# Attention into a feed-forward layer on one Trainium2 core: filler products taken out between the first scores, the first batch's gain moved behind its centering, and one batch's transposes moved into the next stage

## The chip, the core and the metric

The kernel is written for one core of a Trainium2 chip, and uses five of its instruction streams: TensorE (PE, with its weight loads as PEld), VectorE (DVE), ScalarE (ACT), GpSimd (POOL) and SyncE (SP). POOL does little arithmetic here; its queue issues nearly all loads from memory. SP's queue issues the DMA transposes and the stores. Each stream runs its instructions in the order in which they were written out.

The metric is the device time of one execution in microseconds (us). All times given here are of this one core.

## What is computed

```python
# attention: 8 batches, 12 heads, 448 tokens, 64 channels
scores = scale * np.matmul(q, k.transpose(0, 1, 3, 2))
attn = np.maximum(scores, 0.0) ** 2 / S
x = np.matmul(attn, v)                       # then heads side by side: (8, 448, 768)

# feed-forward over d_model = 768, d_ff = 3072
mu = np.mean(x, axis=-1, keepdims=True)
var = np.mean((x - mu) ** 2, axis=-1, keepdims=True)
xn = (x - mu) / np.sqrt(var + 1e-06) * g_ln
out = x + np.maximum(xn @ w_ch1, 0.0) @ w_ch2
```

There is no softmax: a score is clipped at zero and squared. The division by the deviation is a factor of a token, so the kernel takes it out of both products and multiplies with `rstd` at the end; what enters the first product is only the centred x times the gain g.

## The kernel before

**Tiling.** A pair is two heads (128 channels); a batch has six pairs, numbered on over all batches (pair 6 is the first of batch 1). Scores of a pair come in four blocks of 128 keys: `att_QK(i, t)` for t = 0, 1, 2 has 128 keys for both heads, and t = `NF` = 3 has the last 64 keys of pairs i and i+1 together, so two pairs take seven calls. Each call writes a score bank (`sc`, two of them) on PE, then ACT clips it into a buffer `attn` (line 292, seven buffers), then `att_square` squares it on DVE (line 295). `att_AV(i, half)` multiplies with v in two halves of two blocks each (line 314), and its second half ends with an evacuation, which scales into `xT` (line 321 on DVE, or 319 on ACT). q and k of batches 0 and 1 are transposed by PE (`att_T`, line 229, evacuated at line 266); those of later batches by a DMA transpose on SP's queue (line 253).

**Stages.** For each batch b in turn: FFN1(b), 24 tiles `ffn_1(ni)` of 12 products each (line 392) whose result ACT clips into `h` (line 394); then FFN2(b). The attention of batch b+1 is cut into *excursions* of three score calls, placed between the tiles of FFN1(b). An excursion begins with the `att_AV` of a finished pair. Before FFN1(0) comes an opening stage, `step_fine` for pairs 0 and 1, 2 and 3, 4 and 5, and then `first_end`; it does the attention of batch 0. Between its scores it has `warm_up(n)`: n products of 256 columns whose result nobody reads (line 556).

**Centering.** `mean_part(ki)` adds up minus the mean over channels by a product with a constant matrix (line 335). In the opening stage the gain is multiplied right after each evacuation (line 326: on POOL for pairs 0 to 3, on DVE for 4 and 5), and `center_part` adds mean times gain (line 358, DVE). For batch 1 ACT applies the gain (`gain`, line 338) and `center(1)` does the rest, both within `ffn_2_first`.

**FFN1(0) and FFN2(0).** `ffn_1_first` does the first four FFN1 tiles of batch 0 side by side, so that they can begin with the first centred channels (line 663). `ffn_2_first` is FFN2 of batch 0: two token tiles m, two halves dh of the output channels, each sum of 24 inner steps cut into four parts (`plain_part`, line 437). The sums rotate through two banks; a finished one is evacuated by DVE at line 423 and stored at line 416. Also in this stage DVE copies the columns of h that the next batch's first tile shares (`carry`, line 403) and adds up blocks of w2 (`w2_sums`, line 210) for the later batches, whose FFN2 uses seven products in place of eight (line 454, with its operand sums at line 448).

**Transposes of x.** FFN2 adds x in token order. `ffn_x(b, ki)` transposes 128 channels of `xT` into `x_tok` by DMA on SP's queue (line 372), and `ffn_stats` takes mean and variance from `x_tok` (lines 383 to 385, DVE). A batch has 448 tokens, which isn't a whole number of 128-token tiles: batch 1's tiles begin at column 384 of a ring of 896 columns, and so read the last 64 columns of the half that batch 0 and batch 2 use. The evacuation of batch 2's pair into `xT` therefore has to wait until batch 1's transpose of the same channels has been read out.

**Order.** Everything is written out by hand under a manual schedule: the program order of each stream is the order of the calls. On POOL's queue a load waits for the load eight places before it. `load_next` places the loads of w1 parts between the steps of the opening stage.

Of the kernel before, what the change touches and what calls it, by code (L numbers as in the profile page):

```python
# [11 lines left out]
def kernel(  # L12
# [10 lines left out]
    nc = tc.nc  # L23
# [270 lines left out]
    def att_square(i, t):  # L294
        nc.vector.tensor_mul(attn[i, t], attn[i, t], attn[i, t])  # L295

    av = {}

    def xT_of(b, ki):
        return xT[:, ki, (b % 2) * S:(b % 2 + 1) * S]  # L300

    def att_AV(i, half=None, bank=None, evac_by=None):
        b, pr = divmod(i, NPAIR)
        if half != 1:
            av[0] = (next_f() if bank is None else bank)[:, :S]
        ps = av[0]
        v_heads, v_rest = v_parts(b)
        for t in range(NJ) if half is None else range(half * 2, half * 2 + 2):
            for hh in range(2):
                if t < NF:  # L310
                    weights, values = v_heads[:, 2 * pr + hh, t * D:(t + 1) * D], attn[i, t][:, hh, :]
                else:
                    weights, values = v_rest[:, pr, row0(i, hh):row0(i, hh) + D], attn[i - i % 2, NF][:, i % 2, :]
                nc.tensor.matmul(ps[hh * D:(hh + 1) * D, :], weights, values,  # L314
                                 start=(t == 0), stop=(t == NJ - 1))
        if half == 0:
            return
        if evac_by is nc.scalar:
            nc.scalar.mul(xT_of(b, pr), ps, c2)
        else:  # L320
            nc.vector.tensor_scalar(xT_of(b, pr), ps, c2, None, op0=Alu.mult)  # L321
        if i >= PE_T * NPAIR and i % 2 and i + NPAIR < NP_ALL:
            load_v(i - 1 + NPAIR)
        if b == 0:
            eng = nc.gpsimd if pr < NPAIR - 2 else nc.vector
            eng.tensor_scalar(xc[:, pr, :], xT_of(b, pr), g_sb[:, pr:pr + 1], None, op0=Alu.mult)  # L326
        elif pr == 1:
            nc.vector.tensor_add(xs, xT_of(b, 0), xT_of(b, 1))
        elif 1 < pr < NPAIR - 1:
            nc.vector.tensor_add(xs, xs, xT_of(b, pr))  # L330
# [273 lines left out]
    def step_fine(i):  # L604

        att_QK(i, 0)
        att_T(i + 1)
        att_square(i, 0)
        att_QK(i, 1)
        att_square(i, 1)  # L610
        if i:
            att_AV(i - 1, 0)
            warm_up(1)
        else:
            warm_up(4)
        att_QK(i, 2)
        if i:
            att_AV(i - 1, 1)
            mean_part(i - 2)
        else:  # L620
            warm_up(4)
        att_square(i, 2)
        att_QK(i, NF)
        att_square(i, NF)
        if i:
            warm_up(4)
            mean_part(i - 1)
        else:
            warm_up(5)
        att_QK(i + 1, 0)  # L630
        if i + 2 < NPAIR:
            att_T(i + 2)
        else:
            warm_up(5)
        att_square(i + 1, 0)
        load_next()
        att_QK(i + 1, 1)
        att_square(i + 1, 1)
        att_AV(i, 0)
        warm_up(1)  # L640
        att_QK(i + 1, 2)
        att_AV(i, 1)
        att_square(i + 1, 2)
        warm_up(1)

    def first_end():
        i = NPAIR
        mean_part(i - 2)
        att_AV(i - 1, 0)
        att_T(i, nc.scalar.copy)  # L650
        warm_up(2)
        att_AV(i - 1, 1)
        att_QK(i, 0)
        att_QK(i, 1)
        mean_part(i - 1)

    def ffn_1_first():
        f_ps, m_ps = next_f(), next_f()
        tiles = [t[:, :S] for t in (f_ps, m_ps, spare[1], next_sc()[:, 0])]
        for ki in range(K1):  # L660
            center_part(ki, mean0)
            for ni, ps in enumerate(tiles):
                nc.tensor.matmul(ps, w1[:, ki, ni * P:(ni + 1) * P], xc[:, ki, :],
                                 start=(ki == 0), stop=(ki == K1 - 1))
        for ni, ps in enumerate(tiles):
            nc.scalar.activation(h[:, ni, CARRY:], ps, Act.Relu)
        for t in range(2):
            att_square(NPAIR, t)
        excursion(1)
# [4 lines left out]
    T_IN_FIRST = {4: 1, 7: 2, 10: 3, 13: 4, 16: 5}  # L674
    X_AT = (4, 6, 8, 10, 12, 14)
    V_AT = {21: PE_T * NPAIR + 2, 23: PE_T * NPAIR + 4}
    STATS_AT = {0: (18, 21, 23), 1: (15, 18, 21, 23), 2: (6, 9, 12, 15)}
    IN_REST = (1, 4, 7, 10, 13, 16, 19)

    def ffn_1_all(b):  # L680
        ms = tiles_of(b)
        for ni in range(NI0 if b == 0 else 0, K2):
            if b == 0 and ni == NI0:
                ffn_1_first()
            if b == 0 and ni in X_AT:
                ffn_x(b, X_AT.index(ni))
            if b == 0 and ni in V_AT:
                load_v(V_AT[ni])
            ffn_1(ni)
            flush()  # L690
            at = STATS_AT[min(b, 2)][:len(ms)]
            if ni in at:
                ffn_stats(ms[at.index(ni)])
            if b == 1 and ni in SUMS_AT:
                w2_sums(*LATE_SUMS[SUMS_AT.index(ni)])
            if b == 0:
                if ni in IN_FIRST:
                    excursion(3)
                if ni == IN_FIRST[-1] + 3:
                    next_AV(bank=spare[1])  # L700
                if ni in T_IN_FIRST:
                    att_T(NPAIR + T_IN_FIRST[ni])
            elif b < B - 1:
                if ni in IN_REST:
                    excursion(3, **(dict(third=(nc.scalar, nc.vector), evac_by=nc.scalar) if b == 1 else {}))
                if ni == IN_REST[-1] + 3:
                    flush_loads()
                    next_AV(bank=spare[1])

    SUMS_AT = (0, 3, 6, 9, 12, 15)  # L710
    LATE_SUMS = [(o, x, y, op, part)
                 for o, x, y, op in ((B_BOT, B21, B22, Alu.add), (B12, B12, B22, Alu.subtract),
                                     (B21, B21, B11, Alu.subtract)) for part in range(2)]
    def ffn_2_first():
        b = 0
        ffn_rstd(b)
        box = {}
        n = 0
        for dh in range(2):
            for half in range(2):  # L720
                for m, part in [(m, 2 * half + x) for m in range(2) for x in range(2)]:
                    plain_part(b, m, dh, part, 4, box)
                    if n == 1:
                        assert not ready
                        for ki in range(K1):
                            ffn_x(1, ki)
                    if n < K1 - 1:
                        gain(1, n)
                    if n == 3:
                        gain(1, K1 - 1)  # L730
                    if n == 4:
                        gain(1, K1 - 2)
                        for step in center(1):
                            step()
                    if n == 8:
                        carry(b)
                    if n in (9, 10):
                        w2_sums(B_SUM, B11, B22, Alu.add, n - 9)
                    if n in (12, 13):
                        w2_sums(B_TOP, B11, B12, Alu.add, n - 12)  # L740
                    n += 1

    def ffn_2_all(b):
        ffn_rstd(b)
# [30 lines left out]
    with tc.manual_schedule(engines=set(ENGINES)):  # L775
        load_heads(0, [("q", 2, 2), ("k", 2, 2), ("k last", 2, H - 2), ("q", 4, 4), ("k", 4, 4), ("v", 0, 4),
                       ("v last", 0, H), ("q", 8, 4), ("k", 8, 4), ("v", 4, 4), ("v", 8, 4)])
        load_early()
        load_heads(1, [("q", 0, 2), ("k", 0, 2), ("k last", 0, H)])
        load_w1(0)  # L780
        load_heads(1, [("q", 2, 4), ("k", 2, 4)])
        load_w1(1)
        later = [lambda: None,
                 lambda: (load_w1(2), load_heads(1, [("v", 0, H), ("v last", 0, H)])),
                 lambda: (load_heads(1, [("q", 6, 6), ("k", 6, 6)]), load_w1(3), load_w1(4))]

        def load_next():
            later.pop(0)()

        warm_up(17)  # L790
        att_T(0)
        warm_up(5)
        for i in range(0, NPAIR, 2):
            step_fine(i)
        load_w1(5)
        first_end()
        load_w2(B11, 0, 0)
        load_w2(B21, 1, 0)
        load_w2(B12, 0, 1)
        load_w2(B22, 1, 1)  # L800
        nc.gpsimd.memset(qk_ring, 0.0)
        i = PE_T * NPAIR
        load_qk(i)
        load_qk(i + 1)
        load_v(i)
        load_qk(i + 2)
        for b in range(B):
            ffn_1_all(b)
            if b == 0:
                ffn_2_first()  # L810
            else:
                ffn_2_all(b)
        flush()
# [30 lines left out]
```

## Time and profile before

| what | before |
|---|---|
| median of 5 runs | 536.6 us (534.84 to 537.17; two near 534.9, three near 536.9) |
| the profiled execution's own time | 534.9 us |
| its span, first to last instruction | 532.9 us |
| PE busy | 520.9 us, 98% of the span |
| DVE, ACT, POOL busy | 377.2, 274.1, 229.0 us |
| HBM read, written | 51.91 MB, 11.01 MB |

The span is cut into stages by the lines of the timeline: the opening stage runs to 32.48 us, FFN1(0) to 72.92, FFN2(0) to 90.66, FFN1(1) to 131.94; from there on six further batches repeat FFN2 and FFN1 at one pace (FFN1 of batch 2 from 159.8 to 197.5, of batch 3 from 225.2 to 262.9). A row of the timeline gives start and duration in us, the engine (a "q" behind it is its queue issuing a DMA), the line, the operation, what it writes and reads, how many were merged, and in brackets how long its engine had been idle and what ended that.

### The profile page before, as it was taken

To read this page: it belongs to the slowest core of one execution; us is meant where nothing else is said; L and a number is where in the kernel's file an instruction comes from. 1 tells how busy PE (TensorE), PEld (TensorE's weight loads), DVE (VectorE), ACT (ScalarE), POOL (GpSimd) and SP (SyncE) were. 2 spreads that over 40 slices of the span, in tenths; PEclk is the share of its full clock that TensorE was granted. 3 is DMA by queue.
4 is the path that set the end of the run, shared out by engine and by line. 5 is a ranking of instruction groups with operands and counts; after the bars stand their busy time and mean duration, and the time that the engine had idled before them with its cause. 6 is when DMAs were issued, how large, how long until landed. Compare 5 with 4: busy or idle time off the path is not lost.

```text
span 532.9 us, 13760 instructions
## 1 busy us (share of the span) xinstructions
PE 520.9 (98%) x5732; PEld 317.4 (60%) x5732; DVE 377.2 (71%) x660; ACT 274.1 (51%) x443; POOL 229.0 (43%) x259
## 2 busy tenths in 40 slices
PE   9989998989999999999999999999999999999996
PEld 5445567546885556655666556655666556666664
DVE  5866779767876878679684887789595876960264
ACT  6956660867327663176632776366624665234320
POOL 8937216667443574326832277228632000320021
PEclk9999999999999999999999999999999999999999
DMA  9999999999534995559934699469924200240022
GB/s 139 183 175 201 205 199 126 149 160 129 50 85 96 98 115 64 107 86 108 106 53 92 101 101 147 77 73 104 116 53 112 44 18 3 70 110 1 1 62 60
DMA packets 175230, 53.04 MB, mean 100 GB/s; under 512 B 154176, under 2 KB 175168, under 8 KB 175168
## 3 DMA queue, kind: packets, MB, share of 16 engines
q0 software_dynamic: 103552, 25.74, 52.3%
q1 hardware_dynamic: 71088, 26.06, 26.2%
q8 instruction: 45, 0.74, 0.6%
q10 hardware_dynamic: 528, 0.37, 0.2%
q14 instruction: 17, 0.14, 0.1%
HBM read 51.91 MB, written 11.01 MB: 118 GB/s over the span
## 4 chain that ended last, share of the span: by engine, by line
PE 81%; DMA 13%; POOL 3%; ACT 2%; issue 1%; DVE 0%; POOLq 0%; DVEq 0%; ACTq 0%
PE f L392 35%; PE f L454 33%; DMA qk_ring<-in_k_dram 5%; PE f L314 5%; DMA s_sb<-in_v_dram 3%; PE sc L284 3%; DMA w<-in_moe_w_ch_dram 2%; PE f L437 1%; PE f L284 1%; DMA w<-in_q_dram 1%; ACT at L292 1%; PE sc L279 1%; POOL xc L326 1%; DMA qkT_t<-qk_ring 1%; POOL w L201 0%
## 5 line engine op out<-in xcount | busy, mean ns | idle before, releaser
L392 PE MATMUL f<-xc,w 128*64 128x448 bf16 x2256 | 227.0, 354 | 0.3
L392 PEld LDWEIGHTS <-w 128*64 128x64 bf16 x2256 | 125.0, 110 | 93.6 <-issue 18.5
L394 ACT ACTIVATE h<-f 128x448 bf16<-128x448 f32 x188 | 102.6, 546 | 103.5 <-PE f L392 102.1
L454 PE MATMUL f<-w,s_sb 128*64 128x384 bf16 (+2 forms) x1584 | 130.0, 324 | 0.0
L292 ACT ACTIVATE at<-sc 128x896 bf16<-128x896 f32 x120 | 104.6, 916 | 18.5 <-PE sc L284 12.2
L454 PEld LDWEIGHTS <-s_sb 128*64 128x64 bf16 x1584 | 92.3, 110 | 35.1
L295 DVE TENSOR_TENSOR at<-at 128x896 bf16<-128x896 bf16 x168 | 97.0, 621 | 6.4 <-ACT at L292 5.7
L488 POOL TENSOR_TENSOR o_t<-o_t,x_tok 128x384 f32<-128x384 f32 x26 | 24.4, 939 | 157.4 <-ACT o_t L487 133.4
L166 POOL DMA_DIRECT2D qk_ring<-in_q_dram x36 | 44.9, 1246 | 84.4 <-DMA qkT_t<-qk_ring 77.3
L290 DVE TENSOR_SCALAR at<-f 128x448 bf16<-128x448 f32 x89 | 51.5, 617 | 25.3 <-PE f L284 25.3
L448 DVE TENSOR_TENSOR s_sb<-h 128x1536 bf16<-128x1536 bf16 x65 | 64.8, 1013 | 0.0
L487 ACT ACTIVATE o_t<-f,rstd 128x384 f32<-128x384 f32 x26 | 15.1, 581 | 94.7 <-DVE acc L492 46.8
L167 POOL DMA_DIRECT2D qk_ring<-in_k_dram x36 | 53.8, 1495 | 4.6 <-DMA w<-in_moe_w_ch_dram 4.6
L454 PE MATMUL f<-w,h 128*64 128x384 bf16 x624 | 52.9, 326 | 0.0
L168 POOL DMA_DIRECT2D qk_ring<-in_k_dram x36 | 45.3, 1258 | 6.1 <-DMA w<-in_moe_w_ch_dram 6.1
L321 DVE TENSOR_SCALAR xT<-f 128x448 bf16<-128x448 f32 x43 | 26.8, 623 | 29.7 <-PE f L314 29.6
L454 PEld LDWEIGHTS <-h 128*64 128x64 bf16 x624 | 36.6, 110 | 14.5
L314 PE MATMUL f<-at,v_ring 128*64 128x448 bf16 x336 | 40.2, 354 | 0.0
L488 POOL TENSOR_TENSOR acc<-acc,x_tok 128x384 f32<-128x384 f32 x24 | 28.1, 1178 | 22.5 <-ACT acc L487 20.8
L358 DVE SCALAR_TENSOR_TENSOR xc<-f,g_sb,xc 128x448 bf16<-128x448 f32 x48 | 30.1, 675 | 8.9 <-PE f L351 8.8
L178 POOL DMA_DIRECT2D v_ring<-in_v_dram x36 | 32.9, 1223 | 5.3 <-DMA w<-in_moe_w_ch_dram 5.0
L284 PE MATMUL sc<-qkT_t 64*128 64x448 bf16 x206 | 31.3, 356 | 0.2 <-ACT qkT_t L266 0.2
(81 smaller groups left out, 395.6 us busy)
## 6 DMA issues: line engine op xcount, KB each, us to landing
w<-in_moe_w_ch_dram POOLq DMA_DIRECT2D x6, 768.0 KB, 13.6
w<-in_moe_w_ch_dram POOLq DMA_DIRECT2D x4, 1152.0 KB, 27.1
v_ring<-in_v_dram POOLq DMA_DIRECT2D x21, 192.0 KB, 5.1
qk_ring<-in_q_dram POOLq DMA_DIRECT2D x36, 112.0 KB, 4.5
qk_ring<-in_k_dram POOLq DMA_DIRECT2D x36, 96.0 KB, 5.2
out_dram<-o_t SPq DMA_DIRECT2D x9, 168.0 KB, 2.2
out_dram<-o_t SPq DMA_DIRECT2D x9, 144.0 KB, 2.1
out_dram<-acc SPq DMA_DIRECT2D x7, 144.0 KB, 2.1
```

Of the source, the lines that this page charges most:

```text
L167: nc.gpsimd.dma_start(k_to[:, :NF], k[b, heads, :SF].rearrange("x (p t) d -> p t x d", t=NF))
L168: nc.gpsimd.dma_start(k_to[:SS, NF], k[b, 2 * a:2 * a + 2, SF:].rearrange("x s d -> s x d"))
L284: nc.tensor.matmul(by_j(half[hh]), k_of(i, r, t, P), q_of(i, r), start=True, stop=True)
L290: nc.vector.tensor_scalar(at[:, x], half[x], 0.0, None, op0=Alu.max)
L292: nc.scalar.activation(at, ps[:, :, :S], Act.Relu)
L295: nc.vector.tensor_mul(attn[i, t], attn[i, t], attn[i, t])
L314: nc.tensor.matmul(ps[hh * D:(hh + 1) * D, :], weights, values, start=(t == 0), stop=(t == NJ - 1))
L392: nc.tensor.matmul(ps[c * D:(c + 1) * D, :], w1[:, ki, n0:n0 + D], xc[:, ki, :], start=(ki == 0), stop=(ki == K1 - 1))
L394: nc.scalar.activation(h[:, ni, CARRY:], ps, Act.Relu)
L448: nc.vector.tensor_tensor(s_sb[:, n], x, y, op=op)
L454: nc.tensor.matmul(ps[c * D:(c + 1) * D, :d1 - d0], stat[:, ki, c * D:(c + 1) * D], w2[:, slot, ki, d0:d1], start=(start and ki == 0), sto ...
L488: nc.gpsimd.tensor_tensor(o_t, o_t, x_half(m, dh), op=Alu.add)
```

## The change

Five edits, all in the first three stages.

1. **Opening stage.** Of 58 filler products 33 are left: the 22 at the start stay, steps and end have 11 in place of 36. `att_AV` orders its four blocks so that an odd pair begins with the shared last block (`[NF, 0, 1, 2]`), and its halves follow that order. `mean_part` is called behind the block of last keys and not before it. The transposes of pair 6 move from `first_end` into the last step and are evacuated by DVE, no longer by ACT; `first_end` has the two halves of the last `att_AV` around the first scores of pair 6.
2. **Loads.** `load_next` is gone; all loads of w1, v, q and k are issued ahead of the steps, in the same order as before.
3. **Gain.** Only pairs 0 and 1 are multiplied with the gain right away, on DVE; POOL has no gain any more. For channels 2 to 5 `ffn_1_first` adds the mean to `xT` on DVE and then ACT multiplies with the gain.
4. **FFN2(0).** For the first half of output channels the order is now tile by tile (m = 0 with its four parts, then m = 1); the second half keeps its order. Centering of batch 1 is spread over parts 4, 6 and 8 in place of part 4 alone. Of the two block sums of w2, the one that doesn't need the last block comes first. A doubled `gain(1, 4)` is gone.
5. **Batch 1's transposes of x** move from FFN2(0), part 1, to FFN1(1), tiles 4, 6, 8, 10, 12 and 14; its statistics from tiles 15, 18, 21 and 23 to 20, 21, 22 and 23.

```diff
+    GAIN_FIRST = 2
...
-        for t in range(NJ) if half is None else range(half * 2, half * 2 + 2):
+        order = [NF, 0, 1, 2] if i % 2 else [0, 1, 2, NF]
+        for n, t in enumerate(order):
+            if half is not None and n // 2 != half:
+                continue
...
-            eng = nc.gpsimd if pr < NPAIR - 2 else nc.vector
-            eng.tensor_scalar(xc[:, pr, :], xT_of(b, pr), g_sb[:, pr:pr + 1], None, op0=Alu.mult)
+            if pr < GAIN_FIRST:
+                nc.vector.tensor_scalar(xc[:, pr, :], xT_of(b, pr), g_sb[:, pr:pr + 1], None, op0=Alu.mult)
...
             att_AV(i - 1, 0)
-            warm_up(1)
         else:
-            warm_up(4)
+            warm_up(3)
         att_QK(i, 2)
         if i:
             att_AV(i - 1, 1)
-            mean_part(i - 2)
         else:
-            warm_up(4)
+            warm_up(3)
...
         if i:
-            warm_up(4)
+            mean_part(i - 2)
+            warm_up(1)
+        else:
+            warm_up(3)
+        att_QK(i + 1, 0)
+        if i:
             mean_part(i - 1)
-        else:
-            warm_up(5)
-        att_QK(i + 1, 0)
-        if i + 2 < NPAIR:
-            att_T(i + 2)
-        else:
-            warm_up(5)
+        att_T(i + 2)
         att_square(i + 1, 0)
-        load_next()
...
     def first_end():
         i = NPAIR
+        att_AV(i - 1, 0)
+        att_QK(i, 0)
         mean_part(i - 2)
-        att_AV(i - 1, 0)
-        att_T(i, nc.scalar.copy)
-        warm_up(2)
+        att_QK(i, 1)
         att_AV(i - 1, 1)
-        att_QK(i, 0)
-        att_QK(i, 1)
         mean_part(i - 1)
...
         for ki in range(K1):
-            center_part(ki, mean0)
+            if ki < GAIN_FIRST:
+                center_part(ki, mean0)
+            else:
+                nc.vector.tensor_tensor(xc[:, ki, :], mean0, xT_of(0, ki), op=Alu.add)
+                nc.scalar.activation(xc[:, ki, :], xc[:, ki, :], Act.Identity, scale=g_sb[:, ki:ki + 1])
...
-    STATS_AT = {0: (18, 21, 23), 1: (15, 18, 21, 23), 2: (6, 9, 12, 15)}
+    STATS_AT = {0: (18, 21, 23), 1: (20, 21, 22, 23), 2: (6, 9, 12, 15)}
...
-            if b == 0 and ni in X_AT:
+            if b < 2 and ni in X_AT:
                 ffn_x(b, X_AT.index(ni))
...
+    CENTER_AT = (4, 6, 8)
...
-            for half in range(2):
-                for m, part in [(m, 2 * half + x) for m in range(2) for x in range(2)]:
-                    plain_part(b, m, dh, part, 4, box)
-                    if n == 1:
-                        assert not ready
-                        for ki in range(K1):
-                            ffn_x(1, ki)
...
-                        for step in center(1):
-                            step()
...
+            order = [(m, part) for m in range(2) for part in range(4)]
+            if dh:
+                order.sort(key=lambda x: x[1] // 2)
+            for m, part in order:
+                plain_part(b, m, dh, part, 4, box)
...
+                if n in CENTER_AT:
+                    steps[CENTER_AT.index(n)]()
...
+                if n in (9, 10):
+                    w2_sums(B_TOP, B11, B12, Alu.add, n - 9)
+                if n in (12, 13):
+                    w2_sums(B_SUM, B11, B22, Alu.add, n - 12)
```

More of the change, by code (lines that the diff above doesn't have):

```diff
@@ L314, in att_AV @@
                 nc.tensor.matmul(ps[hh * D:(hh + 1) * D, :], weights, values,
-                                 start=(t == 0), stop=(t == NJ - 1))
+                                 start=(n == 0), stop=(n == NF))
         if half == 0:
@@ L639, in step_fine @@
         att_AV(i, 0)
-        warm_up(1)
         att_QK(i + 1, 2)
@@ L643, in step_fine @@
         att_square(i + 1, 2)
-        warm_up(1)
     def first_end():
         i = NPAIR
+        att_AV(i - 1, 0)
+        att_QK(i, 0)
         mean_part(i - 2)
-        att_AV(i - 1, 0)
-        att_T(i, nc.scalar.copy)
-        warm_up(2)
+        att_QK(i, 1)
         att_AV(i - 1, 1)
-        att_QK(i, 0)
-        att_QK(i, 1)
         mean_part(i - 1)
@@ L717, in ffn_2_first @@
         box = {}
+        assert not ready
+        steps = center(1)
         n = 0
         for dh in range(2):
-            for half in range(2):
-                for m, part in [(m, 2 * half + x) for m in range(2) for x in range(2)]:
-                    plain_part(b, m, dh, part, 4, box)
-                    if n == 1:
-                        assert not ready
-                        for ki in range(K1):
-                            ffn_x(1, ki)
[L727 to L732, printed above, removed]
-                        for step in center(1):
-                            step()
[L735 to L741, printed above, removed]
+            order = [(m, part) for m in range(2) for part in range(4)]
[3 more added lines that the diff above has]
+                plain_part(b, m, dh, part, 4, box)
+                if n < K1 - 1:
+                    gain(1, n)
+                if n == 3:
+                    gain(1, K1 - 1)
+                if n in CENTER_AT:
+                    steps[CENTER_AT.index(n)]()
+                if n == 8:
+                    carry(b)
+                if n in (9, 10):
+                    w2_sums(B_TOP, B11, B12, Alu.add, n - 9)
+                if n in (12, 13):
+                    w2_sums(B_SUM, B11, B22, Alu.add, n - 12)
+                n += 1
     def ffn_2_all(b):
@@ L782 @@
         load_w1(1)
[L783 to L788, printed above, removed]
+        load_w1(2)
+        load_heads(1, [("v", 0, H), ("v last", 0, H), ("q", 6, 6), ("k", 6, 6)])
+        for c in range(3, NCH):
+            load_w1(c)
         warm_up(17)
@@ L794 @@
             step_fine(i)
-        load_w1(5)
         first_end()
```

## The prediction, made before the changed kernel had run

> **What bounds the kernel now.** The page first: PE is busy 98% of the span, at a granted clock of 0.9 or more in every slice, so the end can come earlier only where PE stands still or does work that nobody needs. The table of windows finds these places. Its columns are the busy time of PE, PEld, DVE, ACT and POOL, the clock, and DMA.
>
> ```profile
> core 0: us, PE busy (x) PEld busy (x) DVE busy (x) ACT busy (x) POOL busy (x), PEclk, DMA share, GB/s
> 25.00:30.00 5.00, 4.06 (x43) 1.65 (x41) 3.50 (x6) 2.73 (x4) 4.86 (x5) 1.00 1.52 159
> 30.00:35.00 5.00, 3.92 (x24) 1.68 (x24) 4.21 (x8) 2.45 (x3) 0.85 (x1) 1.00 1.23 198
> 80.00:85.00 5.00, 3.59 (x46) 2.75 (x43) 5.00 (x8) 0.00 (x0) 4.14 (x5) 1.00 1.66 140
> 105.00:110.00 5.00, 3.23 (x32) 1.73 (x28) 2.82 (x4) 2.51 (x6) 0.00 (x0) 1.00 1.45 272
> ```
>
> Three holes: 2.0 us around 30, 1.41 at 82, 1.77 at 108. What surrounds each is in the timeline. The opening stage:
>
> ```profile
> 16.76 6.82 ACT L292 ACTIVATE at<-sc 128x896 bf16<-128x896 f32 x7 [0.20 <-DVE xT L321]
> ...
> 23.78 3.89 ACT L292 ACTIVATE at<-sc 128x896 bf16<-128x896 f32 x4 [0.20 <-DVE xT L321]
> ...
> 27.71 0.61 DVE L321 TENSOR_SCALAR xT<-f 128x448 bf16<-128x448 f32 x1
> ...
> 28.61 0.62 DVE L295 TENSOR_TENSOR at<-at 128x896 bf16<-128x896 bf16 x1
> ...
> 30.60 0.62 DVE L321 TENSOR_SCALAR xT<-f 128x448 bf16<-128x448 f32 x1 [1.38 <-PE f L314]
> ```
>
> ACT clips scores nearly without a stop from 7.16 to 27.67 and is the stage's pace; PE's busy time here is partly filler. The last square starts 0.9 behind the last clip, since DVE evacuates pair 4 first, and pair 5 is evacuated only at 30.60. The end of FFN2(0):
>
> ```profile
> 78.64 3.64 DVE L358 SCALAR_TENSOR_TENSOR xc<-f,g_sb,xc 128x448 bf16<-128x448 f32 x6 [3.62 <-PE f L351]
> ...
> 82.86 7.99 PE L437 MATMUL f<-w,h 128*64 128x384 bf16 x96 [1.41 <-DVE o_t L423]
> ...
> 85.41 3.88 DVE L210 TENSOR_TENSOR w<-w 128x2304 bf16<-128x2304 bf16 x3
> ...
> 91.00 0.60 DVE L423 SCALAR_TENSOR_TENSOR o_t<-f,rstd,x_tok 128x384 f32<-128x384 f32 x1
> ```
>
> PE waits 1.41 for a bank, because its evacuation stands behind six centerings. But DVE then has no hole from 78.64 to 91.60. And SP's queue, whose rows are issue times:
>
> ```profile
> 82.10 10.24 SPq L253 DMA_TRANSPOSE qkT_t<-qk_ring  x3
> 92.39 8.18 SPq L372 DMA_TRANSPOSE x_tok<-xT  x6
> 100.67 5.93 SPq L416 DMA_DIRECT2D out_dram<-o_t  x8
> 106.77 21.89 SPq L253 DMA_TRANSPOSE qkT_t<-qk_ring  x6
> ```
>
> The fourth q/k transpose (pair 15) is issued at 106.77 behind six transposes of x and eight stores; PE waits for it from about 108.3 to 110.14.
>
> **Opening stage.** 21 clips at 917 ns are 19.26 us; they took 20.51. The other 1.25 are gaps in which PE was late with the next scores. A step of PE (first scores of pair 3 to those of pair 5) runs from 17.37 to 24.39: 7.02 for seven clips of 6.42 together. In it lie three single fillers at 0.22 (19.09 to the scores at 19.31) and a block of four at 0.45; one stays, so PE needs about 7.02 - 0.9 = 6.1, less than ACT. DVE's step is eleven operations at a pitch of 0.55 (18.41, 18.95), 6.05, plus 0.34 for one gain: just below ACT too, with POOL's arithmetic, beside which one square took 1089 ns against 615, out of its way. I leave 0.4 of the gaps, for the two slots that hold a mean and transposes: the last clip ends at 26.8, not 27.68. Behind it the evacuation of pair 4 is already done, its gain is gone, pair 6's transposes and the waiting mean are off the path: square 26.9 to 27.5, AV at 27.55, evacuation 0.61 later (29.99 to 30.60), 28.16. From that evacuation to the first centering was 1.15 (30.60 to 31.75) and to the first FFN1 product 0.73 more: 30.04, against 32.48. **Gain 2.4.**
>
> Added: channels 2 to 5 pass DVE and then ACT. The add has no row; nearest is the centering, 674 ns at a pitch of 607 (bounds: 0.62, as the clip of one PSUM block at line 290, to 0.69). ACT's gain is 4.14 / 7 = 0.59. Channel 2 is ready at 29.31 + 2 x 0.607 + 0.67 + 0.07 + 0.62 = 31.88; PE, at 0.757 for four products, wants it at 31.55. That is 0.3 once; later channels come every 0.61 and are used every 0.757. **Net -2.1**, bounds -1.2 (fillers only took PE's waiting time, so clips keep their pace, and the tail alone gains) to -2.8.
>
> The loads lose POOL's four gains (6.9 us) in between, but their order is the same and POOL waits for earlier loads either way, up to 80.34 for the last w2 block; hidden, 0. That block is first used in part 12 of FFN2(0), near 82.5. FFN1(0) moves as a whole; a w1 part that POOL sees landed at 53.44 is used after 56.
>
> **FFN2(0).** The bank wait goes, since tile 0's evacuation now stands ahead of centering. What is late next is DVE: its run of 12.96 has one evacuation (0.55) fewer behind the mean, which comes after the same five parts, now at 76.4; and it must wait about 0.4 for tile 1's last part. Its last evacuation ends near 76.5 + 12.4 + 0.4 = 89.4, against 91.60, which is the 2.1 already counted. FFN1(1)'s second tile needs that bank: PE stops twice for 0.7 at the stage's start in place of 1.41 at 82. **-0.1**, bounds -1.4 (a bank comes free earlier) to +0.2.
>
> **SP's queue.** The first three q/k transposes stay where the loads put them (to 92.34). Then come the stores, 8 x 0.5 to 0.74, one transpose of x from about 97, and pair 15's transpose from about 98.5. The landing of line 253 has a median of 4.3: 103, where PE wants it at 108.3 - 2.2 = 106.1. The hole of 1.77 goes; 0.2 comes back, because ACT had caught up in it. **-1.6.**
>
> A new wait: batch 2's evacuation into `xT` (line 319 on ACT, 102.86, now 100.6) must wait for batch 1's transpose of the same channels, and behind it on ACT are the clips of scores and FFN1 tiles, for which PE's banks wait. Its landing: 97 + 3.3 (as 106.77 to PE's 110.14) = 100.3, just in time; by the extremes that the view of line 372 gives for batches 0 to 2, 2.3 to 8.6 us, it is 99.3 to 105.6. I take the nearest, 0 cost; bounds 0 to +5. The later channels have 1 us or more of slack.
>
> **Statistics.** Four sets at 1.25 now follow the last excursion, whose squares end at 129.2, with one evacuation of 0.57: 134.4 to 134.8 against 132.83. From there to the end of the first operand sum is 1.40 (134.23): 135.8 to 136.2. The third product of FFN2(1) wants it at 131.94 + 2 x 1.95 = 135.84. **+0.2**, bounds 0 to 0.6.
>
> **Sum.** -2.1 - 0.1 - 1.6 + 0.2 = -3.6. Against the profiled execution's 534.9 that gives 531.3. This execution was among the two fast ones of five; their mean is 536.1 and their median 536.6. The changed kernel's runs should scatter likewise, so I take the mean less 3.6: **532.5**.
>
> [...] The trace grants a clock of 1.00 in all four windows above, three of them with PE a fifth or more idle. [...] After the change PE has, between 26.9 and 30.04, only one AV and one mean, some 0.9 us of work in 3.1; the row of before that is nearest, 106.5 to 110, had half of 3.5 busy and kept its clock. [...]
>
> **Rivals**, on the mean of 536.1:
> - *DVE doesn't bind* at the end of FFN2(0), and the 1.41 is gained whole: 531.2. For it: some of DVE's copies may shorten. Against: its unbroken run.
> - *The opening stage keeps its pace*: -2.2 or so remains: 533.9. For it: fillers fill time in which PE waits. Against: the 0.1 gaps of ACT behind nearly each clip.
> [...]
> - *Slower*: ACT stands at line 319 for batch 1's transposes, as said. At the longest landing, 8.6, ACT stops 5.0 us in the third excursion, and PE with it, for its banks: 536.1 - 3.6 + 5.0 = 537.5. It decides once the first transpose of x lands later than 100.6 + 3.6 = 104.2. Against: the long landings had up to five transposes ahead of them.
>
> **How the numbers follow.** Forecast 0.55; DVE not binding 0.12; opening stage 0.11; clock 0.10; ACT waiting 0.12. A measurement here can tell about 0.3%, 1.6 us, from no change. The forecast and the first rival are beyond that save a tenth of it, the second and third about six times in ten: faster 0.74. Slower is most of the last: 0.11; the rest 0.15. The range takes the bounds of the forecast (-2.8 - 1.6 - some of 1.4 at one end, -1.2 and a short ACT wait at the other): 529.5 to 535.5.
>
> **What would show it.** Right: clips ending near 26.8 and the first product of line 663 near 30.0; no wait at line 437, but PE waiting for line 423 at the start of FFN1(1); no wait at line 279 for line 253; a third product of FFN2(1) hardly late; clock 1.00 throughout. Wrong: a wait of line 319 on line 372, a clock below 1 between 26 and 36, or the last evacuation of FFN2(0) well ahead of PE.

## The result, and the profile after

The changed kernel takes **533.34 us** (median of 43 runs, 530.02 to 537.00), the kernel before 536.02 (80 runs, 532.49 to 538.64): a ratio of **0.9955, 95% interval 0.9943 to 0.9968**. The profiled execution took 533.51, with a span of 531.7, where that of before had 532.9. Line numbers are now those of the changed kernel: 284, 292 and 295 stay, 319, 335, 358, 372, 392, 416, 423, 437 and 663 are now 324, 340, 363, 377, 397, 421, 428, 442 and 664.

The same four windows as before:

```profile
core 0: us, PE busy (x) PEld busy (x) DVE busy (x) ACT busy (x) POOL busy (x), PEclk, DMA share, GB/s
25.00:30.00 5.00, 3.27 (x24) 1.24 (x23) 3.77 (x8) 2.78 (x4) 2.06 (x3) 1.00 1.36 174
30.00:35.00 5.00, 4.85 (x28) 2.27 (x28) 3.13 (x6) 3.46 (x7) 0.83 (x1) 1.00 1.24 198
80.00:85.00 5.00, 5.00 (x64) 3.48 (x62) 5.00 (x6) 0.00 (x0) 4.56 (x5) 1.00 1.60 152
105.00:110.00 5.00, 4.74 (x32) 2.69 (x31) 3.05 (x4) 3.68 (x7) 4.02 (x5) 0.66 1.88 200
```

The hole at 82 is gone, and the row from 30 is nearly full. But the last row has a clock of 0.66: PE is busy because it is slow. The timeline shows the gain first, at the end of the opening stage:

```profile
24.25 1.73 ACT L292 ACTIVATE at<-sc 128x896 bf16<-128x896 f32 x2 [0.40 <-PE sc L284]
...
26.22 1.80 ACT L292 ACTIVATE at<-sc 128x896 bf16<-128x896 f32 x2 [0.24 <-PE sc L284]
...
27.60 0.62 DVE L326 TENSOR_SCALAR xT<-f 128x448 bf16<-128x448 f32 x1 [0.71 <-PE f L319]
...
29.40 0.73 PE L664 MATMUL f<-xc,w 128*128 128x448 bf16 x3 [0.78 <-DVE xc L363]
```

The last clip of batch 0 ends at 25.98 (24.25 + 1.73; the two at 26.22 are already pair 6's) where it ended at 27.67, the last evacuation of the stage is at 27.60 where it was at 30.60, and the first FFN1 product at 29.40 where it was at 32.48. Two clips with nothing between them take 1.73 together here, as two do in the trace of before:

```profile
31.19 1.73 ACT L292 ACTIVATE at<-sc 128x896 bf16<-128x896 f32 x2 [0.46 <-PE sc L284]
```

FFN2(0) starts at 70.33 (before 73.11) and ends with DVE's run:

```profile
79.26 1.27 DVE L363 SCALAR_TENSOR_TENSOR xc<-f,g_sb,xc 128x448 bf16<-128x448 f32 x2
80.44 1.48 DVE L408 COPY h<-h 128x2304 bf16<-128x2304 bf16 x2
81.84 3.88 DVE L210 TENSOR_TENSOR w<-w 128x2304 bf16<-128x2304 bf16 x3
...
87.44 0.60 DVE L428 SCALAR_TENSOR_TENSOR o_t<-f,rstd,x_tok 128x384 f32<-128x384 f32 x1
```

The last evacuation of the stage starts 3.56 earlier than before (87.44 against 91.00). Then, in FFN1(1), SP's queue:

```profile
81.65 9.49 SPq L253 DMA_TRANSPOSE qkT_t<-qk_ring  x3
91.23 5.08 SPq L421 DMA_DIRECT2D out_dram<-o_t  x8
96.36 1.47 SPq L377 DMA_TRANSPOSE x_tok<-xT  x1
98.01 1.57 SPq L253 DMA_TRANSPOSE qkT_t<-qk_ring  x1
```

ACT's row of the same timeline:

```profile
104.62 0.54 ACT L324 ACTIVATE xT<-f 128x448 bf16<-128x448 f32 x1 [5.56 <-DMA x_tok<-xT]
```

And PE's, three of its rows:

```profile
98.23 0.95 PE L319 MATMUL f<-at,v_ring 128*64 128x448 bf16 x8
...
105.22 4.20 PE L397 MATMUL f<-xc,w 128*64 128x448 bf16 x24 [4.11 <-ACT xT L324]
109.23 0.95 PE L319 MATMUL f<-at,v_ring 128*64 128x448 bf16 x8
```

The same two `att_AV` in the kernel before:

```profile
101.82 0.95 PE L314 MATMUL f<-at,v_ring 128*64 128x448 bf16 x8
...
107.08 0.95 PE L314 MATMUL f<-at,v_ring 128*64 128x448 bf16 x8
```

The first transpose of batch 1's x goes out at 96.36, behind the eight stores, and by the trace it lands at 104.52, 8.2 us later. ACT stands 5.56 for it, and PE 4.11 behind ACT, since nobody empties its banks. From 105.12 the trace then grants half the clock for 3.41 us (PEclk 0.50 from 105.12 to 108.53). The AV of the third excursion starts 3.6 us earlier than before (98.23 against 101.82), that of the fourth 2.2 later (109.23 against 107.08). FFN2(1) starts at **131.94 in both profiles**: all that was gained up to 98 is given back within one stage.

From there to the last instruction the profiles of this case need 399.8 us (that of the changed kernel) to 401.0 (that of before). PE's last product ends 395.8 us after that start in every one; what differs is how the last stores go out, in code that no edit touches. So the start of FFN2(1) is the yardstick of the experiments below.

The medians still differ by 2.7. The runs fall into groups by their mean clock: of the changed kernel's the 8 with 0.999 or more take 530.5 on average, the 17 with 0.997 or 0.998 532.7, and the 15 with 0.993 or 0.994 534.8 (four more have 0.995 or 0.990). One stretch of 3.41 us at half the clock lowers the mean over 531 us by 0.003, so by estimate these are runs with none, one and two such stretches. The kernel before has such groups too: of its 97 runs beside the experiments below, the 35 with 0.999 or more take 534.0 and the 54 with 0.997 or less 536.9. At a full clock, then, the changed kernel is about 3.5 ahead (2.9 to 3.7 by the chip that before ran on), but fewer than a fifth of its runs have that, against more than a third of before's. The two traces are one of before at 0.999 and one of the changed kernel at 0.997. That ACT's wait differs from run to run and makes these groups is likely, but no second execution of the changed kernel was traced.

### The profile page after: what moved, and what is told of

Its sections match the earlier page's. It is cut to its first block, busy times and chain, and to the rows that moved or that the text cites. A ratio compares the mean times of both kernels' runs of the same rounds, so it can differ in the third digit from the quotient of the medians.

```text
span 531.7 us, 13700 instructions
## 1 busy us (share of the span) xinstructions
PE 519.1 (98%) x5707; PEld 314.7 (59%) x5707; DVE 375.6 (71%) x661; ACT 273.6 (51%) x445; POOL 221.9 (42%) x255
## 4 chain that ended last, share of the span: by engine, by line
PE 89%; DVE 4%; ACT 3%; DMA 2%; issue 1%; SPq 0%; ACTq 0%; DVEq 0%
PE f L397 39%; PE f L459 33%; PE f L319 6%; PE sc L284 4%; ACT at L292 2%; DMA x_tok<-xT 2%; PE f L442 1%; PE f L284 1%; DVE at L295 1%; PE sc L279 1%; PE f L561 1%; PE f L229 1%; DVE w L210 1%; DVE xT L326 1%; PE f L356 0%
## 5 line engine op out<-in xcount | busy, mean ns | idle before, releaser
L292 ACT ACTIVATE at<-sc 128x896 bf16<-128x896 f32 x120 | 103.3, 916 | 16.0 <-PE sc L284 12.9
L295 DVE TENSOR_TENSOR at<-at 128x896 bf16<-128x896 bf16 x168 | 95.8, 616 | 10.8 <-ACT at L292 10.5
L363 DVE SCALAR_TENSOR_TENSOR xc<-f,g_sb,xc 128x448 bf16<-128x448 f32 x44 | 27.9, 676 | 6.0 <-PE f L356 5.5
## 6 DMA issues: line engine op xcount, KB each, us to landing
w<-in_moe_w_ch_dram POOLq DMA_DIRECT2D x4, 1152.0 KB, 26.8
```

Source lines behind the costliest of these rows:

```text
L292: nc.scalar.activation(at, ps[:, :, :S], Act.Relu)
```

## Experiments

**Theory A**: the opening stage and FFN2(0) gain about 3.5 us, but batch 1's transposes of x, issued in FFN1(1) behind the stores, land after ACT's evacuation into `xT` needs them, which costs a wait and then a stretch at half the clock. **Rivals**: the gain itself is not there; the transposes' landing is long for another reason than their place in SP's queue; the fillers had no part in the gain.

| kernel | FFN2(1) starts | span | time over before, 95% interval |
|---|---|---|---|
| before | 131.94 | 532.9 | |
| changed | 131.94 | 531.7 | 0.9955 (0.9943 to 0.9968) |
| three transposes early | 128.14 | 527.9 | 0.9925 (0.9899 to 0.9951) |
| changed, transposes not moved | 132.17 | 532.0 | 1.0006 (0.9981 to 1.0032) |
| before, only transposes moved | 134.29 | 534.9 | 0.9994 (0.9973 to 1.0014) |
| before, only the opening changed | 135.89 | 535.8 | 0.9996 (0.9975 to 1.0017) |
| before, only FFN2(0) changed | 130.45 | 531.1 | 0.9985 (0.9952 to 1.0017) |
| stores held back | 128.32 | 528.1 | 0.9857 (0.9816 to 0.9899) |
| fillers put back | 131.22 | 531.9 | 0.9966 (0.9934 to 0.9997) |
| no fillers in the steps | 134.58 | 534.4 | 0.9975 (0.9942 to 1.0007) |
| stores on ACT's queue | 138.53 | 538.4 | 1.0027 (1.0006 to 1.0048) |
| stores held, two transposes first | 126.36 | 526.2 | 0.9839 (0.9810 to 0.9868) |

The start of FFN2(1) and the span are of one execution each, the ratio of all.

**1. Three transposes early.** The first three of batch 1's transposes are issued within FFN1(0), the other three stay:

```diff
+            if b == 0 and ni in (9, 12):
+                ffn_x(1, (9, 12).index(ni))
...
+        if i == 9:
+            ffn_x(1, 2)
...
-            if b < 2 and ni in X_AT:
+            if b == 0 and ni in X_AT or b == 1 and ni in X_AT[3:]:
```

> The changed kernel with the first three of batch 1's transposes of x issued within FFN1(0), ahead of the q/k transposes on SP's queue, the other three within FFN1(1). Theory A (what the change gained by 98 us is lost because ACT's evacuation at line 324 waits for the first of these transposes, and the clock falls after that wait): ACT waits less than 0.5 us there, no window of half clock in FFN1(1), FFN2(1) starts near 128.5 us instead of 131.9, and the time is 3 to 4 us below before. Rival B (FFN1(1) is tied to the stream of loads, so whatever is gained ahead of it is lost there in one wait or another): FFN2(1) starts at 131 or later, and the time is that of the changed kernel, about 2.7 below before.

ACT's wait is gone, the clock is 1.00 from 95 to 120, and FFN2(1) starts 3.8 us earlier than in the changed kernel. Not free, though: PE waits 0.45 for a block of w2 at 82.69, and 1.15 at 90.21 and 1.06 at 106.43 for q/k transposes, none of which the changed kernel's profile has there.

**2. Transposes not moved.** The changed kernel with edit 5 taken back:

```diff
-    STATS_AT = {0: (18, 21, 23), 1: (20, 21, 22, 23), 2: (6, 9, 12, 15)}
+    STATS_AT = {0: (18, 21, 23), 1: (15, 18, 21, 23), 2: (6, 9, 12, 15)}
...
-            if b < 2 and ni in X_AT:
+            if b == 0 and ni in X_AT:
...
+                if n == 1:
+                    for ki in range(K1):
+                        ffn_x(1, ki)
```

> The changed kernel without its fifth edit: batch 1's transposes of x back in FFN2(0), part 1, its statistics back at tiles 15, 18, 21, 23. Theory A: SP's queue then holds pair 15's transpose until 105 to 106 as in before, while PE comes 3.7 us earlier; PE waits 4 to 5 us at line 279 for it, FFN2(1) starts at 131 to 132, and the time is within 1 us of before. Rival C (the opening's gain is independent of the transposes): FFN2(1) starts near 128.5, and the time is 3 to 4 us below before.

The timeline of this kernel shows SP's queue as in before, six transposes and eight stores ahead of pair 15's,

```profile
82.20 7.53 SPq L253 DMA_TRANSPOSE qkT_t<-qk_ring  x3
89.78 8.17 SPq L377 DMA_TRANSPOSE x_tok<-xT  x6
98.04 5.83 SPq L421 DMA_DIRECT2D out_dram<-o_t  x8
104.11 6.19 SPq L253 DMA_TRANSPOSE qkT_t<-qk_ring  x3
```

and PE's row of this kernel's timeline, where it waits for pair 15:

```profile
107.94 0.58 PE L279 MATMUL sc<-qkT_t 64*64 64x448 bf16 x2 [3.69 <-DMA qkT_t<-qk_ring]
```

The wait of 1.80 has become 3.69, a little less than the 4 to 5 expected. FFN1(1)'s second tile had started 4.1 earlier than before (87.66 against 91.80), so the wait takes about half of the gain; the rest goes in the stretch from 106.47, where the trace grants half the clock for 6.8 us (0.65 on average from 105 to 110, 0.67 from 110 to 115). The edits before FFN1(1) bring no time without one that lets the transposes come sooner.

**3. Only the transposes moved**: the opposite, edit 5 alone in the kernel before.

> The kernel before with the fifth edit alone. Theory A: the hole of 1.8 us at line 279 goes, but ACT's evacuation of the first pair of batch 2, due at 102.9, waits for a transpose that lands at 103 to 105: 0.5 to 2 us, so the time is within 1 us of before. If the move by itself is a gain, as the prediction had it: 1.4 to 1.6 us below before, without such a wait.

The first transpose goes out at 97.44, ACT waits 3.07 at line 319, more than expected, and PE 1.56 and 1.16 behind it; from 108.78 the clock is halved for 3.4 us (0.88 on average from 105 to 110, 0.78 from 110 to 115). Without the earlier gain edit 5 swaps one wait for another.

**4. Only the opening changed** (edits 1 to 3 in the kernel before).

> The kernel before with edits 1 to 3 alone (opening stage, loads, gain). The first product of FFN1 at 29.4 as in the changed kernel, FFN1(1) starts 2.8 us earlier than before, at 87.9. Theory A: then PE waits 4 to 5 us at line 279 for pair 15's transpose and the time is within 1 us of before. Rival C: 2.5 to 3 us below before.

The first FFN1 product is at 29.73, so the gain of the stage is there; PE then waits 5.40 at line 279 in this profile (111.24), has half the clock for 6.8 us from 110.61 (0.56 on average from 110 to 115, 0.76 from 115 to 120), and the time is that of before.

**5. Only FFN2(0) changed** (edit 4 in the kernel before).

> The kernel before with the part for FFN2(0) alone (tile by tile in the first half, one block of centering behind the norm vector, sums in the other order). Theory A: the wait of 1.41 at line 437 goes, FFN1(1)'s second tile comes 0.5 to 1 earlier, since DVE binds the end of the stage, and PE then waits 2.3 to 2.8 at line 279 for pair 15's transpose instead of 1.77: FFN2(1) starts where it started before, within 0.3, and the time is within 1 us of the kernel before. Rival (the 1.41 is gained for good): FFN2(1) starts 1 us or more earlier, and the time is 1.4 under.

The 1.41 at line 437 goes. From the start of FFN2(0) to FFN1(1)'s second tile it takes 18.13 (72.34 to 90.47) against 18.69 before: 0.56 gained, near what theory A gave. FFN2(1) starts 1.5 earlier, which A did not give, but 0.8 of that was there before FFN2(0) began, since this execution's opening, with unchanged code, ended at 31.72 and not 32.48. By time the kernel can't be told from before, and PE's wait at line 279 was 1.52, not the 2.3 to 2.8 that A expected, since pair 15's transpose went out earlier too (105.32 against 106.77). So for A, against its rival, only the 0.56 speaks.

**6. Stores held back.** SP's eight stores of FFN2(0) issued in tile 17 of FFN1(1):

```diff
-            store(o_t, m, dh * HD, (dh + 1) * HD)
+            held.append(lambda: store(o_t, m, dh * HD, (dh + 1) * HD))
...
+            if b == 1 and ni == 17:
+                for put in held:
+                    put()
```

> The changed kernel with the eight stores of FFN2(0) held back and issued in tile 17 of FFN1(1), behind the transposes. Theory A (the six transposes of batch 1's x were late because SP's queue has the stores ahead of them, so that the first goes out at 96.4 and ACT's evacuation into xT waits 5.6 us): the first transpose goes out near 91.5 and lands near 95 to 98, before ACT wants it at 98.5; no wait at line 324, the clock stays at 1.00 between 95 and 120, FFN2(1) starts near 128.3 where the changed kernel has 131.94, and the time is 3.5 to 5 us under the kernel before. Rival (the landing takes 8 us whatever is ahead in SP's queue, since loads of POOL's queue move at that time): a wait of 2 us or more stays at line 324, and the time is that of the changed kernel, about 2.5 under the kernel before.

Its timeline, SP's queue:

```profile
81.71 9.08 SPq L253 DMA_TRANSPOSE qkT_t<-qk_ring  x3
90.84 1.63 SPq L377 DMA_TRANSPOSE x_tok<-xT  x1
95.82 1.24 SPq L253 DMA_TRANSPOSE qkT_t<-qk_ring  x1
97.11 1.65 SPq L377 DMA_TRANSPOSE x_tok<-xT  x1
```

ACT's first two evacuations into `xT` in the same kernel:

```profile
99.34 0.55 ACT L324 ACTIVATE xT<-f 128x448 bf16<-128x448 f32 x1 [0.15 <-PE f L319]
...
106.59 0.54 ACT L324 ACTIVATE xT<-f 128x448 bf16<-128x448 f32 x1 [2.20 <-DMA x_tok<-xT]
```

The first transpose goes out at 90.84 and lands at 96.48, and ACT now waits for PE there. FFN2(1) starts at 128.32, where A had 128.3. The time fell by 7.9 (528.23 against 536.09), more than the 3.5 to 5 expected: that figure left out that the changed kernel was itself 2.7 under before; what remains is not accounted for. The second transpose, issued at 97.11, still took 9.4 us, with no store ahead of it, so ACT waits 2.20 for it. That much of the rival came true: near 97 a landing is long with or without the stores. What holding them back does is that the first transpose goes out 5.5 us earlier.

**7. Stores held, two transposes first**: both of the first two ahead of pair 15's transpose.

```diff
...
+            if b == 1 and ni in X_AT[:-1]:
+                for ki in ((0, 1) if ni == X_AT[0] else (X_AT.index(ni) + 1,)):
+                    ffn_x(b, ki)
...
```

> The kernel with held stores, with each transpose of batch 1's x from the second on issued one slot earlier, the first two together in tile 4 of FFN1(1), ahead of pair 15's transpose. Theory A: the second goes out near 92.5 and lands near 98 to 101, so ACT's wait of 2.20 at 106.59 and PE's of 1.17 behind it go, and FFN2(1) starts near 127.1; the time is 1 us under that of the held stores. Rival (pair 15's transpose, now behind one more, lands later): PE waits 0.5 to 2 us longer at line 279 near 105, and the time is that of the held stores or up to 1 us more.

SP's queue in the timeline of this kernel:

```profile
82.33 7.79 SPq L253 DMA_TRANSPOSE qkT_t<-qk_ring  x3
90.17 2.76 SPq L377 DMA_TRANSPOSE x_tok<-xT  x2
96.33 1.23 SPq L253 DMA_TRANSPOSE qkT_t<-qk_ring  x1
```

and ACT's second evacuation into `xT`:

```profile
104.64 0.54 ACT L324 ACTIVATE xT<-f 128x448 bf16<-128x448 f32 x1 [0.15 <-PE f L319]
```

The two land at 95.99 and 97.21. PE has no gap over 0.15 us left in FFN1(1) after its second tile, and FFN2(1) starts 5.6 us earlier than in either original kernel. With 527.83 us (536.55 before, in the same runs) this is the lowest of all; from experiment 6 it can't be told apart by time, since the intervals of the two ratios overlap. Pair 15's transpose landed at 104.45, and nobody waits for it.

**8. Stores on ACT's queue**, at their old moments, so that they are neither ahead of the transposes nor held.

```diff
-            store(o_t, m, dh * HD, (dh + 1) * HD)
+            store(o_t, m, dh * HD, (dh + 1) * HD, (nc.scalar,))
```

> The changed kernel with the eight stores of FFN2(0) issued by ACT, at the same moments as before, instead of SP. Theory A (the place in SP's queue decides when batch 1's transposes land): the first transpose of x goes out near 91, as in the kernel with held stores, and lands near 96.5; at most 0.5 us of PE's time is lost to line 324 at its first wait, the clock stays at 1.00 from 95 to 110, FFN2(1) starts within 1 us of 128.3, and the time is 6.5 to 8 us under the kernel before. Rival (the bytes of the stores, which move at the same time as the transposes in this kernel, delay them whatever queue they are in): the first transpose lands at 101 or later, PE loses 2 us or more at line 397 to ACT, FFN2(1) starts at 130 or later, and the time is 2.5 to 4.5 under the kernel before.

ACT's rows in this kernel's timeline:

```profile
81.55 17.74 ACTq L421 DMA_DIRECT2D out_dram<-o_t  x6
99.39 0.98 ACT L399 ACTIVATE h<-f 128x448 bf16<-128x448 f32 x2 [18.61 <-DMA x_tok<-xT]
```

and PE's:

```profile
88.93 1.33 PE L397 MATMUL f<-xc,w 128*64 128x448 bf16 x12 [0.28 <-DVE o_t L428]
...
99.99 6.31 PE L397 MATMUL f<-xc,w 128*64 128x448 bf16 x36 [7.26 <-ACT h L399]
```

A miss: neither theory foresaw it. The last four stores leave at 89.84, 91.66, 97.74 and 98.97, each within 0.08 us after one of SP's transposes has landed (89.77, 91.64, 97.66, 98.95). So on ACT a store waited for an earlier transpose, and ACT's clips waited behind the store: the first tile of FFN1(1) was done at 90.26, its clip began at 99.39, 9.1 us later (the rest of the 18.61 is time in which ACT had nothing to do), and PE stood 7.26 us. The first transpose of x went out at 92.99 and landed at 98.95, but with PE and ACT standing this tells little of the two theories.

**9 and 10. Fillers.** The changed kernel with the 25 fillers put back (58 in all), and with none but the 22 ahead of the first scores.

> The changed kernel with the 25 filler products that it took out of the opening put back, in the same places, its other orders kept. Theory A (the fillers stood in PE's way to the next scores, so that ACT's clips waited): the last clip of the opening ends 0.7 to 1.5 later than the changed kernel's, and its first FFN1 product is near 30.4 instead of 29.40. Rival (fillers only fill time in which PE waits anyway): the first FFN1 product is within 0.2 of 29.40. The time of either is about that of the changed kernel, since what comes earlier is lost again at line 324.

> The changed kernel without any filler in the steps of the opening (the 22 ahead of the first scores stay). By the trace (PE a fifth to a third idle, in pieces of at most 1.5 us, has kept its clock): clock 1.00 from 8 to 36 and the first FFN1 product at 29.1 to 29.4. [...]

The windows of the kernel with fillers back:

```profile
25.00:30.00 5.00, 4.80 (x45) 1.80 (x43) 3.04 (x6) 3.46 (x5) 2.06 (x3) 1.00 1.38 171
30.00:35.00 5.00, 3.71 (x11) 1.42 (x11) 4.56 (x9) 2.41 (x5) 0.83 (x1) 0.66 1.24 198
```

and of the kernel without:

```profile
5.00:10.00 5.00, 3.67 (x54) 2.04 (x49) 2.81 (x6) 3.72 (x5) 4.48 (x8) 1.00 1.50 152
10.00:15.00 5.00, 4.42 (x46) 1.51 (x40) 3.45 (x8) 3.39 (x5) 4.48 (x7) 0.66 1.45 149
```

With fillers back the first FFN1 product is at 31.64, 2.24 later than in the changed kernel and more than the 30.4 expected; the last clip of batch 0 ends at 27.83 and not at 25.98. The clock falls only at 31.65, so this is the fillers' own cost. Seven profiles with the changed opening and its own fillers have it at 29.03 to 30.21, three with the old opening at 31.72 to 32.48: the fillers are most of the difference. By the start of FFN2(1) this kernel is level with the changed one all the same: it comes later to the same transposes, so ACT waits only 1.69 at line 324, and PE 0.24 and 1.17 behind it. Without fillers PE stood in pieces of at most 0.56 us, and still the clock fell at 11.23 for 3.4 us (0.66 in the row from 10), and the first product came at 30.47. The expectation failed on both counts, though PE was not idle ahead of the fall: it was busy for 1.96 us of the 3.41 before it.

## Why the prediction was right, and where it was not

The mechanism of the gain and the forecast of faster held; the measured median lies 0.8 over the predicted time. That agreement is in part luck, for two errors stand behind it and partly cancel: up to FFN1(1) the gain was 1.5 larger than thought, and a wait that was taken as 0 cost PE 4.1, and then 3.41 us at half the clock.

- **Opening stage**, -2.1 by the prediction. The first FFN1 product came 3.1 earlier, FFN1's next tile 2.8 (34.64 against 37.41); executions of one and the same opening differ by 0.8 to 1.2. The term that was too small is the pace of the clips. The last one of batch 0 ended at 25.98 and not at 26.8; from there to the first product it took 3.4, near the 3.2 of the sum. The sum took 917 ns for every clip, but two that follow each other without a wait take 1.73 together and not 1.83, in both traces (rows at 24.25 and 31.19 above), so the second begins about 0.82 after the first. Putting the fillers back takes 2.24 of the 3.1 away in the execution traced, which speaks against the rival by which the opening keeps its pace; the other edits of the stage (order of blocks, loads, gain) were not tried apart. That rival's number has a slip: with the bound of -1.2 given for it the sum is -2.7, so 533.4 and not 533.9. That the median lies at 533.34 doesn't make it right.
- **Channel 2's detour** over ACT, 0.3: its first product is at 31.23, where the pitch before it would have given 30.16 + 0.76 = 30.92. Right.
- **Loads, statistics**, 0 and +0.2: FFN2(0) starts 2.8 earlier, as FFN1's next tile did, with no wait for w2; the third product of FFN2(1), for which 135.84 was worked out as the due time, starts at 135.84. The statistics cost 0.
- **FFN2(0)**, -0.1: FFN1(1)'s second tile starts at 88.09 and not 91.80, 3.7 earlier, where 2.8 had been gained by the start of the stage. The reasoning held (DVE binds; PE waits 0.47 for line 428 at the start of FFN1(1)), but the term for DVE's copies was off: the two copies of `h` took 1.48 (80.44 to 81.92) and not 2.24 as in the trace of before (83.25 to 85.49). Why they are shorter was not tried.
- **SP's queue**, -1.6: the hole at line 279 went. Pair 15's transpose landed at 105.27, though, not at 103; nobody waits for it only because PE was already standing for ACT.
- **The new wait**, taken as 0 with bounds up to +5: **this step failed.** It put the landing at "97 + 3.3 (as 106.77 to PE's 110.14) = 100.3, just in time". It was 104.52, past the 104.2 from which the slower rival was to decide; ACT's wait was 5.56, PE's 4.11. Experiments 6 and 7 show that its place behind the stores is what makes it late: issued at 90.2 to 91.6 the transposes land 5.6 to 5.8 us later, in time. The 3.3 was taken from a q/k transpose issued at 106.77, when the last transfer already under way landed 2.38 us later (a store, 109.15); at 96.36 loads of v were under way whose last landed 8.35 us later (104.71). Nearer rows were in the same trace: the six transposes of x in the kernel before, issued from 92.4 to 99.3, took 5.0 to 8.4 us, beside the same loads of v. The prediction set them aside because "the long landings had up to five transposes ahead of them"; here one with none under way ahead of it took 8.2. Its slower rival had this very case, a landing of 8.6 and a stop of 5.0 for ACT, and its list of signs of being wrong had this wait; the trace shows that mechanism, and the run was faster all the same because the gain ahead was larger and, it seems, because many runs lose less.
- **The clock**, 0: in this profile it was 1.00 in the thin stretch at 28, as forecast, with PE busy for only 1.68 us of the 3.41 from 26.18. In the kernel with fillers back PE had more work, 1.92 us from 28.23 to 31.65, and there the clock fell. So how much PE works in such a stretch did not tell which of the two comes, and one row of before with half of 3.5 us busy was little ground for counting no loss. The chances have a fall of the clock in the thin stretch as a rival of its own, with 0.10; no run shows what it would have cost there. What the runs showed is a price elsewhere, behind ACT's wait, where the prediction had no term for it: the 3.41 us from 105.12 held 3.27 us of PE's work at half the clock, so they cost about 1.6. The groups of runs above lie 2.1 to 2.2 apart, but may contain differences of the wait too.

In the profiled pair, then, 3.6 gained up to the third excursion and 1.8 of the old wait stand against 4.1 of the new one and about 1.6 of half clock; runs in which ACT waits less presumably keep the rest.

**Left open**: what sets a landing time near 97. Transposes issued between 96.0 and 98.1 landed at 103.45 to 106.51 in every kernel whose profile has such, with stores ahead of them or without; all that time the loads of v from POOL's queue were landing as well (in the changed kernel one at 104.33 and one at 104.71, both issued before the transpose, which landed at 104.52). Whether it is these loads that hold the transposes up was not shown; a kernel without the loads was not tried. That ACT's wait differs from run to run is read from the runs' times and clocks, not from further traces. Open, too, is the scatter of the kernel before, 532.5 to 538.6, of which only one execution was traced. In that trace the clock is 1.00 all through the hole at line 279, with PE busy for 1.61 us of the 3.41 from 107.50. Whether the 54 of 97 runs at 0.997 or less lose clock there, and what closing that hole is worth in them beyond the 1.6 of the prediction, was not shown: none of them was traced.

## What to carry to other kernels

When a transfer is moved to a place where something waits for it, take its landing time from transfers issued in the same microseconds beside the same loads, not from a kinder row elsewhere (here 5.0 to 8.4 us, against the 3.3 that was taken), and count what stands ahead of it in its own queue and what is already under way. Stores that nobody waits for belong behind the transposes that somebody waits for (here the first transpose went out 5.5 us earlier for it). A gain made ahead of a fixed wait is not a gain until that wait moves too: the opening, FFN2(0) and the moved transposes, each alone, changed nothing here that could be measured, nor did all but the moved transposes together.

## What the runs showed of the hardware

- In the changed kernel the clock is 0.50 from 105.12 to 108.53, 3.41 us, and 1.00 behind that. Worked out from the means of 5 us windows, half the clock lasted 3.4 us with fillers back (from 31.65), in the opening without fillers (from 11.23) and with only the transposes moved (from 108.78), 6.8 us with the transposes not moved (from 106.47) and with only the opening changed (from 110.61), and 10.2 us with the stores on ACT's queue (0.53, 0.50 and 0.95 from 95 to 110).
- What PE did just ahead of it differs much: no work in the 3.42 us before 105.12 (changed kernel), 1.92 us in the 3.42 before 31.65 (fillers back), 1.96 in the 3.41 before 11.23, with no gap over 0.56 us (no fillers). The clock also stayed at 1.00 with less than the last two: 1.61 us of work in the 3.41 from 107.50 (before) and 1.68 in the 3.41 from 26.18 (changed kernel). What decides between the two was not shown.
- With the stores on ACT's queue four of them left within 0.08 us after a transpose of SP's had landed, and ACT's arithmetic stood behind them: the clip of a tile that was done at 90.26 began at 99.39, 9.1 us later.
- One and the same opening stage, with the same code, ends up to 0.8 us apart in three profiles (31.72 to 32.48) and up to 1.2 in seven (29.03 to 30.21).
